# Expert products spread among the attention's small products, by a planner that counts TensorE's instructions, and a second buffer for the next pair's gram blocks

## The chip, the cores and the metric

One Trainium2 chip, one of its cores. The metric is the time of one execution on the device in microseconds; each time given for a kernel is the median of several runs.

## What is computed

Three layers follow each other on 4 x 768 = 3072 tokens. Everything is float32.

```python
def _attn_ref(q, k, v, beta):            # 4 batches, 8 heads, 768 steps, 48 wide
    k_n = k / (np.linalg.norm(k, axis=-1, keepdims=True) + 1e-06)
    for t in range(S):
        y[:, :, t] = np.einsum('bhd,bhde->bhe', q[:, :, t], state)
        v_old = np.einsum('bhde,bhd->bhe', state, kt)
        state = state + bt[:, :, :, None] * np.einsum('bhd,bhe->bhde', kt, vt - v_old)

def _moe_ref(x, w_gate, w1, w2):         # 3072 x 384, 8 experts, 1024 wide
    logits = x @ w_gate
    P = np.exp(logits - logits.max())
    for _ in range(8):
        P /= P.sum(1, keepdims=True) + 1e-09
        P /= P.sum(0, keepdims=True) + 1e-09
        P *= N / E
    for e in range(E):
        out += P[:, e:e + 1] * (np.maximum(x @ w1[e], 0.0) @ w2[e])

def _moe2_ref(x, w1, w2, w3, w_out):     # 3072 x 384, 1024 wide
    return (((x @ w1) * (x @ w2)) @ w3) @ w_out
```

## The kernel before

**Attention.** The 768 steps are cut into 12 chunks of 64, and two chunks make a pair. For a chunk, the products within it are computed at once for all 32 heads, in groups of small products that are packed four at a time into TensorE's array. `quads` (L494) issues such a group: 32 calls, which the chip executes as 64 matmuls with 64 weight loads. A chunk has seven groups:

- `gram` (L472): keys by keys, for the triangular system of the chunk. ScalarE and VectorE write its blocks into "a" (tile `a0`, L484 and the scalar_tensor_tensor after it) and "g" (tile `g12`).
- `pmm` (L648): keys by queries, masked by VectorE into "pt".
- `ks` and `qs` (L696, L705): the state by keys and by queries. `qs` starts the sum in PSUM that `pu` ends.
- `um` (L711): the inverse by the values; ScalarE writes "u". `um2` (L724): the new state; ScalarE writes "st". `pu` (L732): the output of the chunk, which goes through `xst` and DRAM (`xs_d`) and comes back token by token as `xr`.

The system of a pair is inverted by VectorE (`invert`, L507): a transposition into `asys` (L518), 14 small steps, 24 products and sums over up to 1024 columns, and a transposition of the result `t` back into `asys` (L578). Then `tt_make` (L583) forms the off-diagonal blocks: `xm` (L601) multiplies "g" with the inverse, ScalarE writes it back into the other half of "g", and `om` (L622) multiplies that once more; each is 16 calls per half chunk, executed as 32 matmuls. `gram` of the next pair writes "g" again, of which there is one buffer (`NG12 = 1`), so it comes after `om` of the pair before. The state goes from chunk to chunk through ks, um and um2.

**Expert 0.** While the attention runs, the first expert is already applied to the chunks that are finished (`e0`, L772): 24 products m1 (`xr` by the first weights) and 24 products m2 (`hA` by the second) per chunk, each of three matmuls of 128 x 128 by 256 columns. ScalarE and VectorE write `hA` (relu, split into two parts for precision), in tiles of two blocks, four buffers. The router's logits (`lg`, `lt2`) belong to each chunk as well. After the last chunk, `sinkhorn` (L901) does its eight rounds on VectorE, each with one small matmul for the sum over partitions.

**The rest.** Experts 1 to 7 follow in three passes over the tokens (`unit`, L982, with `hB` and `hA`), then the third layer (`phase_c`). Both hold TensorE with products of 512 or 384 columns.

**The order.** Nothing of this is executed in the order in which it is written. The program's operations are collected by `Plan.op` with a cost per engine, a priority and the keys that they read and write; `Plan.order` (L139) then steps through a model of the engines, takes at each moment the operation of the best priority that could start, and writes out one fixed order. `e0`'s products have priority 200 + chunk, the attention's groups -100 + chunk, the preparation of a pair (gram, inversion, xm, om, pmm) 10 times the pair and a little more. So expert products are taken where no attention operation is ready. The costs are constants of the source: `QUAD = .12` us for four calls of a group, `act` and `dve` for ScalarE and VectorE by columns. An operation marked `low` (xm, om) is put back when much of that kind ran just before.

SP's queue issues most loads and stores (L365) in the planned order: keys (`kt`), queries (`qt`, three buffers, `NQ = 3`), values, the way of the outputs through DRAM, and the stores of expert 0's results (`yr`).

Of the kernel before, what the change touches and what calls it, by code (L numbers as in the profile page):

```python
# [12 lines left out]
ALU = mybir.AluOpType  # L13
# [13 lines left out]
NKN = 2  # L27
NQ = 3
NA0 = 2
# [15 lines left out]
NC0 = 11  # L45
NG12 = 1
QUAD = .12
FLAT = "p a b c d -> p (a b c d)"
# [24 lines left out]
class Op:  # L73
    __slots__ = ("engs", "fn", "prio", "preds", "succs", "npred", "slots", "est", "rdy", "low", "start", "end", "eng", "lat", "nbytes", "hook")


class Plan:
# [14 lines left out]

    def op(self, engs, fn, r=(), w=(), prio=0.0, lat=0.0, nbytes=0, hook=None, low=False):
        o = Op()
        o.hook = hook
        o.low = low
        o.engs, o.fn, o.prio, o.lat, o.nbytes = engs, fn, (prio, len(self.ops)), lat, nbytes
# [24 lines left out]
        return o  # L122

    AHEAD = .2
    LOWMAX = 1.2
    URGENT = 2.0

    def wait_for(self, o, e, pool, now, room):
# [10 lines left out]
    def order(self):  # L139
# [11 lines left out]
        warm = {}  # L151
        lows = []

        def cost_of(o, e):
# [4 lines left out]
            if k not in warm:  # L159
# [6 lines left out]
                warm[k] = w  # L166
            return o.engs[e] * (1.0 if warm[k] else self.COLD)

        def crowded():
# [23 lines left out]
        while pool:  # L193
# [6 lines left out]
            for o in pool:  # L200
# [87 lines left out]
def act(n, psum=False):  # L288
    return (n / 1.2 + (55 if psum else 95)) / 1000

# [21 lines left out]
class Kernel:  # L312
# [123 lines left out]
    def prep_k(self, c):  # L436
# [13 lines left out]
        if st:  # L450
# [15 lines left out]
            g.op({"DVE": 1.3}, newton, r=n0 + ["bm"], w=["n1", ("bm", j), ("nv", j)], prio=pr)  # L466
        gi = j % NG12
        if st == 0:
            self.a0[j] = self.aring.new()
        sg = [self.psum.new("attn") for _ in range(2)]  # L470

        def gram(e):  # L472
            kt = lambda r, x, y, m: T["kt"][r, k.at, 8 * y + m]
            self.quads([self.ps(s, 8, 64) for s in sg], kt, kt, lambda x, y: (x, y, x), rows=D)
        g.op({"PE": 8 * QUAD}, gram, r=[k], w=sg + [(self.a0[j], "z")] + [
            (n, gi, st, hf) for n in ("g12", "xsb0", "xsb1") for hf in range(2)], prio=pr)
        for hf in range(2):
# [5 lines left out]
            g.op({"ACT": act(256, True)}, lambda e, s=s, ss=ss, a0=a0: self.copy(  # L483
                "ACT", T["a0"][:, a0.at, ss], self.ps(s, 8, 64)[:, :, 0:32], T["masks"][:, 64:65]), r=[s, "masks"], w=[ak], prio=pr)  # L484
            g.op({"ACT": act(256, True)}, lambda e, s=s, gs=gs, st=st: self.copy(
                "ACT", T["g12"][:, gi, st, gs], self.ps(s, 8, 64)[:, :, 32:64], -1.0),
                r=[s], w=[(n, gi, st, hf) for n in ("g12", "xsb0", "xsb1")], prio=pr)
            g.op({"DVE": dve(256)}, lambda e, s=s, ss=ss, a0=a0: self.stt(
                T["a0"][:, a0.at, ss], self.ps(s, 8, 64)[:, :, 32:64], T["masks"][:, 65:66], T["a0"][:, a0.at, ss], ALU.mult, ALU.add),
                r=[s, "masks", ("g12", gi, st, hf)], w=[ak], prio=pr)  # L490

# [91 lines left out]
    def tt_make(self, c):  # L583
# [8 lines left out]
        for hf in range(2):  # L592
# [15 lines left out]
            g.op({"PE": 16 * .027}, xm, r=[("g12", gi, st, hf), "asys"], w=[s], prio=pr, low=True)  # L608
            for b in range(2):
# [19 lines left out]
            g.op({"PE": 16 * .043}, om, r=[("xsb0", gi, st, hf), ("xsb1", gi, st, hf), tk(1)], w=[s2], prio=pr, low=True)  # L629
            for b in range(2):  # L630
# [5 lines left out]
    def prep_q(self, c):  # L636
# [14 lines left out]
        g.op({"PE": 8 * QUAD}, pmm, r=[q, k], w=sp + [(self.PT[c, hf], "z") for hf in range(2)], prio=pr)  # L651
        for hf in range(2):
# [15 lines left out]
    def seq(self, c):  # L668
# [24 lines left out]
        if c > 0:  # L693
            sk = two()

            def ks(e):  # L696
                self.quads([self.ps(s, 8, D) for s in sk], lambda r, x, y, m: T["kt"][r, k.at, 8 * y + m],
                           lambda r, x, y, m: T["st"][r, px.at, 8 * (x ^ y) + m], lambda x, y: (x, y, x), rows=D)
            g.op({"PE": 8 * QUAD}, ks, r=[k, (px, 0), (px, 1)], w=sk, prio=pr)
            for hf in range(2):  # L700
# [13 lines left out]
        g.op({"PE": 8 * QUAD}, um, r=vk + [(tt, hf, i) for hf in range(2) for i in range(3)] + [("qs", c)], w=su, prio=pr)  # L714
        for hf in range(2):
# [3 lines left out]
        if c < NCH - 1:  # L719
# [7 lines left out]
            g.op({"PE": 8 * QUAD * .8}, um2, r=uk + [kr], w=ss, prio=pr)  # L727
            for hf in range(2):
# [43 lines left out]
    def e0(self, c):  # L772
# [7 lines left out]
        for f0 in range(0, EB, 2):  # L780
# [4 lines left out]
            for fi in range(n):  # L785
                for kk in range(3):
                    def m1(e, kk=kk, s=s, f=f0 + fi, fi=fi):
# [113 lines left out]
    def sinkhorn(self):  # L901
# [4 lines left out]
        op("DVE", 0.0, lambda e: None, [("lgr", t) for t in range(NCH)], ["p"])  # L906
        op("DVE", .3, lambda e: nc.vector.tensor_reduce(out=cs()[:, 0:1], in_=p(), axis=AX.XY,
                                                        op=ALU.max), ["p"], ["cs"])
# [8 lines left out]
                                                        op0=ALU.mult), [s2], ["cs"])  # L917
        op("ACT", .4, lambda e: nc.scalar.activation(out=p(), in_=p(),
                                                      func=AF.Exp, bias=cs()[:, 1:2]), ["cs"], ["p"])
        for it in range(8):  # L920
            op("DVE", .3, lambda e: nc.vector.tensor_reduce(out=rs(), in_=T["p"][:, 0:NTT], axis=AX.X, op=ALU.add), ["p", "eps"], ["rs"])
            op("DVE", .1, lambda e: nc.vector.reciprocal(out=rs(), in_=rs()), [], ["rs"])
            op("DVE", .3, lambda e: self.tt("DVE", p(), p(), rs().rearrange("p (t o) -> p t o", o=1).to_broadcast([128, NTT, NE]),
                                            ALU.mult), ["rs"], ["p"])
            op("DVE", .3, lambda e: nc.vector.tensor_reduce(out=cs(), in_=T["p"][:, :, 0:NE].rearrange("p t e -> p e t"), axis=AX.X,
                                                            op=ALU.add), ["p", "eps"], ["cs"])
            s = self.psum.new("attn")
            op("PE", .2, lambda e, s=s: self.mm(self.ps(s, NE), T["ones"], cs(), start=True, stop=True), ["cs", "ones"], [s])
            op("DVE", .1, lambda e, s=s: nc.vector.reciprocal(out=cs(), in_=self.ps(s, NE)), [s], ["cs"])
            op("DVE", .3, lambda e: self.stt(p(), p(), float(NT) / NE, cs().rearrange("p (o e) -> p o e", o=1).to_broadcast(  # L930
                [128, NTT, NE]), ALU.mult, ALU.mult), ["cs"], ["p"])
# [528 lines left out]
```

## Time and profile before

| | |
|---|---|
| median of 3 runs | 2201.05 us (2196.92 to 2206.56) |
| the profiled execution, time | 2200.67 us |
| its span, first to last instruction | 2198.9 us |
| TensorE busy | 2064.0 us (94%) |
| VectorE, ScalarE, GpSimd busy | 1250.1, 716.2, 833.4 us |
| attention, expert 0 and sinkhorn, to the first product of expert 1 | 0 to 490.3 us |
| experts 1 to 7 | 490.3 to 1917 us |
| third layer | 1917 to 2198.9 us |

In rows of the profile PE is TensorE's matmuls, PEld its weight loads, DVE VectorE, ACT ScalarE, POOL GpSimd, SP the queue of SyncE. Times are microseconds from the start of the span. "PEclk" is the granted clock of TensorE as a share of 2.4 GHz; at 0.5 it runs at 1.2 GHz. Nearly all matmuls have the line L334, that of a helper, so they are told apart by what they read: `kt` alone is gram, `qt,kt` pmm, `st,kt` ks, `qt,st` qs, `vs,tt` um, `u,kraw` um2, `pt,u` pu, `asys,g` xm, `tt,g` om, `xr,wA` m1, `hA,wA` m2, `xr,wg` and `masks,yr` the logits, `cs,ones` the sinkhorn's sums, `xT,...` expert 1 and later.

### The profile page before, as it was taken

How to read it: one execution, taken by the hardware profiler on the slowest of the kernel's cores; microseconds unless marked ns; L12 is line 12 of the kernel's file. 1: busy time of each engine (PE TensorE's matmuls, PEld its weight loads, DVE VectorE, ACT ScalarE, POOL GpSimd, SP SyncE). 2: the span in 40 equal slices, each digit the busy share in tenths (PEclk: the TensorE clock that was granted, in tenths of full speed). 3: DMA queues.
4: the chain of work that ended last, by engine and by line, in shares of the span. 5: the costliest groups of instructions: out<-in, count | busy, mean ns of one | idle time of the engine just before them, and what ended most of it. 6: DMA issues, size and time to landing. Idle time of an engine off the chain costs nothing.

```text
span 2198.9 us, 39139 instructions
## 1 busy us (share of the span) xinstructions
PE 2064.0 (94%) x16017; PEld 1761.6 (80%) x16017; DVE 1250.1 (57%) x1957; ACT 716.2 (33%) x1387; POOL 833.4 (38%) x893
## 2 busy tenths in 40 slices
PE   2889998888999899989999999999999999999999
PEld 1878887876888787778887788788887888988888
DVE  7867765553545555576666766767667644222222
ACT  3433333333344334333233233323322322222222
POOL 3200000034766856754546544634466434300000
PEclk9899978899999999999999999999999999999999
DMA  6432131135555555684556445555655545700000
GB/s 218 156 106 72 64 96 53 41 104 199 204 195 191 182 178 201 210 286 164 206 201 232 163 176 199 199 179 196 211 206 172 206 142 164 139 29 30 15 15 30
DMA packets 165461, 331.61 MB, mean 151 GB/s; under 512 B 13280, under 2 KB 117664, under 8 KB 153760
## 3 DMA queue, kind: packets, MB, share of 16 engines
q1 hardware_dynamic: 131392, 193.82, 26.8%
q0 software_dynamic: 33888, 135.28, 17.9%
q8 instruction: 126, 2.06, 0.4%
q14 instruction: 55, 0.45, 0.1%
HBM read 235.10 MB, written 93.95 MB: 150 GB/s over the span
## 4 chain that ended last, share of the span: by engine, by line
PE 78%; DVE 6%; issue 5%; POOL 4%; DMA 4%; ACT 2%; SPq 1%; POOLq 0%; DVEq 0%; ACTq 0%
PE b L334 78%; DMA rawB<-in_moe_w 2%; DVE prod L345 1%; POOL acc L345 1%; POOL wA L345 1%; SPq L365 1%; POOL wS L345 1%; POOL rawB L345 1%; DVE cv L348 1%; DVE t L544 0%; DVE xs L544 0%; DMA xst<-xs_d 0%; DMA wA<-wq_d 0%; ACT rt L338 0%; DVE hA L348 0%
## 5 line engine op out<-in xcount | busy, mean ns | idle before, releaser
L334 PE MATMUL b<-hA,wA 128*128 128x512 f32 (+1 forms) x2367 | 502.9, 354 | 5.9 <-DVE hA L348 3.5
L334 PEld LDWEIGHTS b<-hA,wA 128*128 128x128 f32 x2367 | 392.9, 191 | 67.1 <-DVE hA L348 4.7
L334 PE MATMUL b<-hB,wA 128*128 128x512 f32 x1521 | 391.5, 393 | 2.3 <-DVE hB L348 2.3
L345 POOL TENSOR_TENSOR acc<-acc,tmp 128x512 f32<-128x512 f32 x252 | 331.2, 1316 | 160.4 <-DVE tmp L345 157.6
L334 PEld LDWEIGHTS b<-hB,wA 128*128 128x128 f32 x1521 | 288.1, 189 | 63.6 <-DVE hB L348 3.5
L334 PE MATMUL b<-xr,wA 128*128 128x256 f32 (+1 forms) x1620 | 326.9, 340 | 0.0
L334 PEld LDWEIGHTS b<-xr,wA 128*128 128x128 f32 x1620 | 255.1, 195 | 31.6 <-DVE b L345 0.4
L345 DVE TENSOR_TENSOR tmp<-b,pb 128x512 f32<-128x512 f32 x234 | 161.0, 689 | 200.1 <-PE b L334 192.4
L338 ACT ACTIVATE rt<-b 128x512 f32<-128x512 f32 x300 | 178.0, 597 | 256.6 <-PE b L334 250.9
L334 PE MATMUL b<-xT,wA 128*128 128x512 f32 x1008 | 253.7, 393 | 6.8 <-ACT wA L338 5.6
L345 DVE TENSOR_TENSOR b<-b,rt 128x512 f32<-128x512 f32 x252 | 173.8, 696 | 125.1 <-ACT rt L338 62.2
L334 PEld LDWEIGHTS b<-xT,wA 128*128 128x128 f32 x1008 | 190.4, 189 | 49.0 <-ACT wA L338 6.4
L334 PE MATMUL b<-xT,wS 128*128 128x512 f32 x756 | 205.0, 396 | 16.7 <-ACT wS L338 9.2
L345 POOL TENSOR_TENSOR cv<-cv 128x256 f32<-128x256 f32 (+3 forms) x175 | 127.7, 730 | 198.9 <-DVE cv L1222 109.6
L334 PEld LDWEIGHTS b<-xT,wS 128*128 128x128 f32 x756 | 141.1, 189 | 55.2 <-ACT wS L338 12.5
L348 DVE SCALAR_TENSOR_TENSOR hA<-b,hA 128x512 fp32r<-128x512 f32 x215 | 144.7, 689 | 58.5 <-ACT hA L1032 41.5
L345 DVE TENSOR_TENSOR rt<-b,rt 128x512 f32<-128x512 f32 x48 | 33.2, 692 | 186.0 <-PE b L334 186.0
L1032 ACT ACTIVATE hB<-b 128x512 fp32r<-128x512 f32 x169 | 100.5, 597 | 108.6 <-DVE b L345 106.0
L348 DVE SCALAR_TENSOR_TENSOR hB<-b,hB 128x512 fp32r<-128x512 f32 x169 | 115.3, 686 | 34.7 <-ACT hB L1032 34.4
L345 POOL TENSOR_TENSOR wA<-rawB,wA 128x768 fp32r<-128x768 f32 (+2 forms) x64 | 95.9, 1507 | 102.4 <-ACT wA L338 76.3
L338 ACT ACTIVATE cv<-cv 128x256 fp32r<-128x256 f32 x72 | 29.2, 405 | 281.8 <-DVE cv L348 281.8
L1032 ACT ACTIVATE hA<-b 128x512 fp32r<-128x512 f32 x167 | 97.6, 597 | 57.9 <-DVE b L345 32.9
(164 smaller groups left out, 2425.3 us busy)
## 6 DMA issues: line engine op xcount, KB each, us to landing
wA<-wq_d POOLq DMA_DIRECT2D x56, 1536.0 KB, 9.2
wq_d<-wA SPq DMA_DIRECT2D x28, 1536.0 KB, 7.0
wS<-ws_d POOLq DMA_DIRECT2D x56, 512.0 KB, 5.7
rawB<-in_moe_w SPq DMA_DIRECT2D x112, 192.0 KB, 4.3
ws_d<-wS SPq DMA_DIRECT2D x28, 512.0 KB, 4.3
w_d<-cv SPq DMA_DIRECT2D x112, 128.0 KB, 2.1
pb<-p_d SPq DMA_DIRECT2D x42, 256.0 KB, 4.2
cvr<-in_w3T SPq DMA_DIRECT2D x32, 256.0 KB, 2.7
```

The source lines that it names most:

```text
L334: self.nc.tensor.matmul(*args, skip_group_check=True, **kw)
L338: self.nc.scalar.activation(out=out, in_=in_, func=AF.Copy, **({} if scale is None else {"scale": scale}))
L345: self.E[eng].tensor_tensor(out=out, in0=in0, in1=in1, op=op)
L348: self.nc.vector.scalar_tensor_tensor(out=out, in0=in0, scalar=scalar, in1=in1, op0=op0, op1=op1)
L365: return self.g.op({eng: cost}, lambda _: e.dma_start(out=out(), in_=in_()), r=r, w=w, prio=prio, nbytes=nbytes, lat=lat)
L1032: g.op({"ACT": actb(512)}, lambda e: nc.scalar.activation(out=hv(0), in_=self.ps(s, 512), func=AF.Relu), r=[s], w=[(out, 0, 0)], prio=pe)
```

## The change

Four things change, all of them ahead of the code that runs on the chip, except two buffers.

1. The planner counts TensorE's instructions. Each operation has a number `ins` (6 unless given: three matmuls and three weight loads; 128 for a group, 32 for xm and om). `fetch` says by how much the instruction that stands 256 further along would come too early, 3.9 us after the one 256 before it. A group (16 instructions or more) that would wait by more than 0.1 us is put back, and the next best operation that can start, in most cases an expert product, is taken. What is late all the same is added to the group's time.
2. `NG12` is 2, and `gram` with the four operations behind it has priority -120 + pair from the second pair on, ahead of the attention. Its place is paid for by the third query buffer (`NQ` 3 to 2).
3. `qs` of a chunk reads a key that `pu` of the chunk before writes, so it stands behind it.
4. Costs are set anew: `QUAD` .12 to .14, 55 ns more for each operation of ScalarE, m1 .33 to .36, the sinkhorn's steps each for itself.

```diff
-NQ = 3
+NQ = 2
...
-NG12 = 1
-QUAD = .12
+NG12 = 2
+QUAD = .14
...
+    BLOCK = 256
+    FETCH = 3.9
...
+        def fetch(o, now):
+
+            if o.ins < 16:
+                return 0.0
+            d = 0.0
+            for x in (0.0, .5, 1.0):
+                i = issued[0] + x * o.ins - self.BLOCK
+                for i0, n, a, b in reversed(stream[-300:]):
+                    if i0 <= i < i0 + n:
+                        d = max(d, a + (b - a) * (i - i0) / n + self.FETCH - now - x * o.engs["PE"])
+                        break
+            return d
...
-                if o.low and full:
+                if o.low and full or e == "PE" and fetch(o, now) > .1:
                     spare = spare or (o, e)
                     continue
...
+            if e == "PE":
+                late = fetch(o, now)
+                end += late
+                stream.append((issued[0], o.ins, now + late, end))
+                issued[0] += o.ins
...
-    return (n / 1.2 + (55 if psum else 95)) / 1000
+    return (n / 1.2 + (110 if psum else 150)) / 1000
...
+        pg = pr if j == 0 else -120.0 + j
...
-        g.op({"PE": 8 * QUAD}, gram, r=[k], w=sg + [(self.a0[j], "z")] + [
-            (n, gi, st, hf) for n in ("g12", "xsb0", "xsb1") for hf in range(2)], prio=pr)
+        g.op({"PE": 8 * QUAD}, gram, ins=128, r=[k], w=sg + [(self.a0[j], "z")] + [
+            (n, gi, st, hf) for n in ("g12", "xsb0", "xsb1") for hf in range(2)], prio=pg)
...
-            g.op({"PE": 8 * QUAD}, qs, r=[q, (px, 0), (px, 1)], w=sy + [("qs", c)], prio=pr)
+            g.op({"PE": 8 * QUAD}, qs, ins=128, r=[q, (px, 0), (px, 1), ("pu", c - 1)], w=sy + [("qs", c)], prio=pr)
...
-        g.op({"PE": 8 * QUAD}, pu, r=uk + pts, w=sy + [(xb, "z")], prio=pr + .2)
+        g.op({"PE": 8 * QUAD}, pu, ins=128, r=uk + pts, w=sy + [(xb, "z"), ("pu", c)], prio=pr + .2)
...
-                    g.op({"PE": .33}, m1, r=xk + [("w", f0 + fi, i) for i in range(2)], w=[s, (h, "z")], prio=pr)
+                    g.op({"PE": .36}, m1, r=xk + [("w", f0 + fi, i) for i in range(2)], w=[s, (h, "z")], prio=pr)
...
-        op("ACT", .4, lambda e: nc.scalar.activation(out=p(), in_=p(),
+        op("ACT", 1.75, lambda e: nc.scalar.activation(out=p(), in_=p(),
```

What this does to the order is seen at two places. On TensorE, in the middle of the attention, the end of um2 and what follows it. Before, it is the next group:

```order
L334 MATMUL b_141<-u,kraw 48x48 x2
L334 MATMUL b_137<-u,kraw 48x48 x2
L334 MATMUL b_141<-u,kraw 48x48
L334 MATMUL b_135<-pt,u 48x64 x2
L334 MATMUL b_134<-pt,u 48x64 x2
```

And with the change, at such a place:

```order
L357 MATMUL b_137<-u,kraw 48x48 x2
L357 MATMUL b_136<-u,kraw 48x48
L357 MATMUL b_134<-xr,wA 128x256 x12
L357 MATMUL b_140<-hA,wA 128x256 x6
L357 MATMUL b_138<-st,kt 64x48 x2
```

Four products m1 and two m2 stand between um2 and ks, where before one group followed the other.

The second place is VectorE's, between the end of one pair's inversion (the transposition of t into asys) and the start of the next (that of a into asys). Before, for the third and the fourth pair ("a<-b" writes the next pair's gram blocks, "vs<-b" follows ks, "tt" are the off-diagonal blocks):

```order
L578 STREAM_TRANSPOSE asys<-t 128x32x32
L580 STREAM_TRANSPOSE a_113<-t 128x32x32
...
L345 TENSOR_TENSOR vs<-vs,nv 128x768
L348 SCALAR_TENSOR_TENSOR vs<-b_138,vs 128x384
L348 SCALAR_TENSOR_TENSOR vs<-b_140,vs 128x384
L348 SCALAR_TENSOR_TENSOR a_113<-b_135,masks,a_113 128x256
L348 SCALAR_TENSOR_TENSOR a_113<-b_136,masks,a_113 128x256
L348 SCALAR_TENSOR_TENSOR a_113<-b_135,masks,a_113 128x256
...
L345 TENSOR_TENSOR xr<-xst,xr 128x768
L348 SCALAR_TENSOR_TENSOR a_113<-b_136,masks,a_113 128x256
L518 STREAM_TRANSPOSE asys<-a_113 128x1024
```

With the change, for the fourth and the fifth pair:

```order
L602 STREAM_TRANSPOSE asys<-t 128x32x32
L604 STREAM_TRANSPOSE a_113<-t 128x32x32
L371 SCALAR_TENSOR_TENSOR hA<-b_139,hA 128x512
L368 TENSOR_TENSOR tt<-a_113,bm 128x8x32 x2
L368 TENSOR_TENSOR tt<-b_139,bm 32x8x32 x2
L368 TENSOR_TENSOR tt<-b_140,bm 32x8x32 x2
L371 SCALAR_TENSOR_TENSOR hA<-b_134,hA 128x512
L368 TENSOR_TENSOR tt<-b_139,bm 32x8x32 x2
L542 STREAM_TRANSPOSE asys<-a_113 128x1024
```

The gram blocks were written during the inversion before; the operations on the state (vs) come after the start of the next one.

## Rows read from the trace of the kernel before

**Rows 1.** Busy time by stretch: from:to, length; each engine (instructions); PEclk, DMA share, GB/s

```profile
50.80:126.10 75.30, 67.14 (x1436) 62.87 (x1436) 65.02 (x118) 30.89 (x68) 12.38 (x7) 0.89 0.39 121
126.10:197.00 70.90, 61.59 (x1460) 58.41 (x1460) 49.31 (x79) 23.84 (x55) 3.58 (x4) 0.93 0.30 88
197.00:269.00 72.00, 65.53 (x1484) 62.31 (x1483) 47.99 (x74) 24.35 (x57) 2.24 (x2) 0.91 0.29 90
269.00:338.00 69.00, 62.75 (x1489) 59.71 (x1488) 49.91 (x75) 24.27 (x57) 3.59 (x3) 0.83 0.26 79
338.00:410.00 72.00, 64.43 (x1474) 60.70 (x1474) 48.03 (x74) 23.85 (x55) 1.65 (x4) 0.91 0.15 46
410.00:490.30 80.30, 67.23 (x1009) 62.16 (x1003) 37.01 (x82) 25.35 (x51) 13.85 (x11) 0.85 0.30 86
...
520.30:1917.00 1396.70, 1368.09 (x5999) 1126.68 (x6000) 837.00 (x1303) 464.87 (x883) 754.74 (x823) 0.99 0.57 193
```

**Rows 2.** Timeline of TensorE, 208 to 229 us: first and last of six stops

```profile
208.15 0.51 PE L334 MATMUL b<-u,kraw 64*48 64x48 f32 x26 [1.02 <-issue]
...
228.72 0.66 PE L334 MATMUL b<-qt,st 48*48 48x64 f32 x29 [0.95 <-issue]
```

**Rows 3.** The page: TensorE's instructions, the instruction queue, loads of qt

```profile
PE 2064.0 (94%) x16017; PEld 1761.6 (80%) x16017; DVE 1250.1 (57%) x1957; ACT 716.2 (33%) x1387; POOL 833.4 (38%) x893
...
q8 instruction: 126, 2.06, 0.4%
...
qt<-in_qT SPq DMA_DIRECT2D x12, 512.0 KB, 5.0
```

**Rows 4.** Timeline of TensorE: operations at full clock, the last at a lower one

```profile
197.01 1.20 PE L334 MATMUL b<-asys,g 32*32 32x32 f32 x64
...
204.36 1.15 PE L334 MATMUL b<-vs,tt 64*64 64x48 f32 x64
205.44 0.69 PE L334 MATMUL b<-tt,g 32*32 32x32 f32 x32
...
229.31 0.87 PE L334 MATMUL b<-xr,wg 128*16 128x256 f32 x6
...
296.88 1.91 PE L334 MATMUL b<-st,kt 48*64 48x48 f32 x64
```

**Rows 5.** Busy time in slices of 10 us, columns as in rows 1

```profile
180.00:190.00 10.00, 10.00 (x86) 10.00 (x85) 9.79 (x10) 2.08 (x5) 0.00 (x0) 1.00 0.12 39
...
290.00:300.00 10.00, 7.86 (x290) 7.23 (x284) 6.20 (x10) 2.69 (x5) 2.40 (x1) 0.50 0.46 140
```

**Rows 6.** Waits of TensorE, 50.5 to 490 us: us in total, times, longest

```profile
PE b L334 <- issue: 36.4, 28, 2.8
...
PE b L334 <- DVE cs L925: 6.7, 5, 2.2
...
PE b L334 <- DMA qt<-in_qT: 0.3, 1, 0.3
```

**Rows 7.** VectorE from one inversion's end to the next start; last, two groups' means

```profile
194.76 2.06 DVE L578 STREAM_TRANSPOSE asys<-t 128x1024 f32<-128x1024 f32 x1
...
217.51 0.48 DVE L348 SCALAR_TENSOR_TENSOR a<-b,masks,a 128x256 f32<-128x256 f32 x1 [3.92 <-ACT g L338]
...
229.62 2.00 DVE L518 STREAM_TRANSPOSE asys<-a 128x1024 f32<-128x1024 f32 x1
...
L348 DVE SCALAR_TENSOR_TENSOR hA<-b,hA 128x512 fp32r<-128x512 f32 x42 | 28.8, 686 | 10.7 <-ACT hA L796 10.5
...
L345 DVE TENSOR_TENSOR prod<-a,xs 128x1024 f32<-128x1024 f32 x18 | 23.5, 1322 | 0.0
```

**Rows 8.** Timeline of TensorE: the last pu, and the sinkhorn's result transposed

```profile
431.28 2.33 PE L334 MATMUL b<-pt,u 64*48 64x64 f32 x64 [0.59 <-ACT u L338]
...
479.98 0.38 PE L1174 MATMUL b<-ident,tmp 128*96 128x128 f32 x2
```

**Rows 9.** Waits of SP's queue, 0 to 450 us: us in total, times, longest

```profile
SPq L365 <- ACT yr L338: 207.0, 21, 22.0
```

More of the change, by code (lines that the diff above doesn't have):

```diff
@@ L73 @@
 class Op:
-    __slots__ = ("engs", "fn", "prio", "preds", "succs", "npred", "slots", "est", "rdy", "low", "start", "end", "eng", "lat", "nbytes", "hook")
+    __slots__ = ("engs", "fn", "prio", "preds", "succs", "npred", "slots", "est", "rdy", "low", "start", "end", "eng", "lat", "nbytes", "hook", "ins")
 class Plan:
@@ L91, in __init__, with op @@
         self.rd = {}
-    def op(self, engs, fn, r=(), w=(), prio=0.0, lat=0.0, nbytes=0, hook=None, low=False):
+    def op(self, engs, fn, r=(), w=(), prio=0.0, lat=0.0, nbytes=0, hook=None, low=False, ins=6):
         o = Op()
@@ L96, in op @@
         o.low = low
+        o.ins = ins
         o.engs, o.fn, o.prio, o.lat, o.nbytes = engs, fn, (prio, len(self.ops)), lat, nbytes
@@ L152, in order @@
         lows = []
+        stream = []
+        issued = [0]
         def cost_of(o, e):
@@ L483, in prep_k @@
             g.op({"ACT": act(256, True)}, lambda e, s=s, ss=ss, a0=a0: self.copy(
-                "ACT", T["a0"][:, a0.at, ss], self.ps(s, 8, 64)[:, :, 0:32], T["masks"][:, 64:65]), r=[s, "masks"], w=[ak], prio=pr)
+                "ACT", T["a0"][:, a0.at, ss], self.ps(s, 8, 64)[:, :, 0:32], T["masks"][:, 64:65]), r=[s, "masks"], w=[ak], prio=pg)
             g.op({"ACT": act(256, True)}, lambda e, s=s, gs=gs, st=st: self.copy(
                 "ACT", T["g12"][:, gi, st, gs], self.ps(s, 8, 64)[:, :, 32:64], -1.0),
-                r=[s], w=[(n, gi, st, hf) for n in ("g12", "xsb0", "xsb1")], prio=pr)
+                r=[s], w=[(n, gi, st, hf) for n in ("g12", "xsb0", "xsb1")], prio=pg)
             g.op({"DVE": dve(256)}, lambda e, s=s, ss=ss, a0=a0: self.stt(
                 T["a0"][:, a0.at, ss], self.ps(s, 8, 64)[:, :, 32:64], T["masks"][:, 65:66], T["a0"][:, a0.at, ss], ALU.mult, ALU.add),
-                r=[s, "masks", ("g12", gi, st, hf)], w=[ak], prio=pr)
+                r=[s, "masks", ("g12", gi, st, hf)], w=[ak], prio=pg)
     TDONE = [("t16", 1, 0), ("t16", 1, 8), ("t16", 0)]
@@ L607, in xm @@
                                 start=True, stop=True, tile_position=(64 * b, 64 * b + 32))
-            g.op({"PE": 16 * .027}, xm, r=[("g12", gi, st, hf), "asys"], w=[s], prio=pr, low=True)
+            g.op({"PE": 16 * .027}, xm, r=[("g12", gi, st, hf), "asys"], w=[s], prio=pr, low=True, ins=32)
             for b in range(2):
@@ L628, in om @@
                                 start=True, stop=True, tile_position=(64 * b + 32, 64 * b))
-            g.op({"PE": 16 * .043}, om, r=[("xsb0", gi, st, hf), ("xsb1", gi, st, hf), tk(1)], w=[s2], prio=pr, low=True)
+            g.op({"PE": 16 * .043}, om, r=[("xsb0", gi, st, hf), ("xsb1", gi, st, hf), tk(1)], w=[s2], prio=pr, low=True, ins=32)
             for b in range(2):
@@ L650, in pmm @@
                        lambda r, x, y, m: T["qt"][r, q.at, 8 * y + m], lambda x, y: (x, x ^ y, x), rows=D)
-        g.op({"PE": 8 * QUAD}, pmm, r=[q, k], w=sp + [(self.PT[c, hf], "z") for hf in range(2)], prio=pr)
+        g.op({"PE": 8 * QUAD}, pmm, ins=128, r=[q, k], w=sp + [(self.PT[c, hf], "z") for hf in range(2)], prio=pr)
         for hf in range(2):
@@ L698, in ks @@
                            lambda r, x, y, m: T["st"][r, px.at, 8 * (x ^ y) + m], lambda x, y: (x, y, x), rows=D)
-            g.op({"PE": 8 * QUAD}, ks, r=[k, (px, 0), (px, 1)], w=sk, prio=pr)
+            g.op({"PE": 8 * QUAD}, ks, ins=128, r=[k, (px, 0), (px, 1)], w=sk, prio=pr)
             for hf in range(2):
@@ L713, in um @@
                        lambda r, x, y, m: T["vs"][r, v.at, 8 * x + m], lambda x, y: (y, x ^ y, y))
-        g.op({"PE": 8 * QUAD}, um, r=vk + [(tt, hf, i) for hf in range(2) for i in range(3)] + [("qs", c)], w=su, prio=pr)
+        g.op({"PE": 8 * QUAD}, um, ins=128, r=vk + [(tt, hf, i) for hf in range(2) for i in range(3)] + [("qs", c)], w=su, prio=pr)
         for hf in range(2):
@@ L726, in um2 @@
                            lambda r, x, y, m: T["u"][r, u.at, 8 * y + m], lambda x, y: (x ^ y, x, x ^ y), cols=D, first=c == 0)
-            g.op({"PE": 8 * QUAD * .8}, um2, r=uk + [kr], w=ss, prio=pr)
+            g.op({"PE": 8 * QUAD * .8}, um2, ins=128, r=uk + [kr], w=ss, prio=pr)
             for hf in range(2):
@@ L906, in sinkhorn @@
         op("DVE", 0.0, lambda e: None, [("lgr", t) for t in range(NCH)], ["p"])
-        op("DVE", .3, lambda e: nc.vector.tensor_reduce(out=cs()[:, 0:1], in_=p(), axis=AX.XY,
+        op("DVE", .37, lambda e: nc.vector.tensor_reduce(out=cs()[:, 0:1], in_=p(), axis=AX.XY,
                                                         op=ALU.max), ["p"], ["cs"])
@@ L917, in sinkhorn @@
                                                         op0=ALU.mult), [s2], ["cs"])
-        op("ACT", .4, lambda e: nc.scalar.activation(out=p(), in_=p(),
+        op("ACT", 1.75, lambda e: nc.scalar.activation(out=p(), in_=p(),
                                                       func=AF.Exp, bias=cs()[:, 1:2]), ["cs"], ["p"])
         for it in range(8):
-            op("DVE", .3, lambda e: nc.vector.tensor_reduce(out=rs(), in_=T["p"][:, 0:NTT], axis=AX.X, op=ALU.add), ["p", "eps"], ["rs"])
-            op("DVE", .1, lambda e: nc.vector.reciprocal(out=rs(), in_=rs()), [], ["rs"])
-            op("DVE", .3, lambda e: self.tt("DVE", p(), p(), rs().rearrange("p (t o) -> p t o", o=1).to_broadcast([128, NTT, NE]),
+            op("DVE", .4, lambda e: nc.vector.tensor_reduce(out=rs(), in_=T["p"][:, 0:NTT], axis=AX.X, op=ALU.add), ["p", "eps"], ["rs"])
+            op("DVE", .32, lambda e: nc.vector.reciprocal(out=rs(), in_=rs()), [], ["rs"])
+            op("DVE", .5, lambda e: self.tt("DVE", p(), p(), rs().rearrange("p (t o) -> p t o", o=1).to_broadcast([128, NTT, NE]),
                                             ALU.mult), ["rs"], ["p"])
-            op("DVE", .3, lambda e: nc.vector.tensor_reduce(out=cs(), in_=T["p"][:, :, 0:NE].rearrange("p t e -> p e t"), axis=AX.X,
+            op("DVE", .54, lambda e: nc.vector.tensor_reduce(out=cs(), in_=T["p"][:, :, 0:NE].rearrange("p t e -> p e t"), axis=AX.X,
                                                             op=ALU.add), ["p", "eps"], ["cs"])
@@ L928, in sinkhorn @@
             op("PE", .2, lambda e, s=s: self.mm(self.ps(s, NE), T["ones"], cs(), start=True, stop=True), ["cs", "ones"], [s])
-            op("DVE", .1, lambda e, s=s: nc.vector.reciprocal(out=cs(), in_=self.ps(s, NE)), [s], ["cs"])
-            op("DVE", .3, lambda e: self.stt(p(), p(), float(NT) / NE, cs().rearrange("p (o e) -> p o e", o=1).to_broadcast(
+            op("DVE", .22, lambda e, s=s: nc.vector.reciprocal(out=cs(), in_=self.ps(s, NE)), [s], ["cs"])
+            op("DVE", .42, lambda e: self.stt(p(), p(), float(NT) / NE, cs().rearrange("p (o e) -> p o e", o=1).to_broadcast(
                 [128, NTT, NE]), ALU.mult, ALU.mult), ["cs"], ["p"])
```

## Prediction

> **What bounds the kernel.** I began with the busy time by stretch [rows 1]. From 520.3 us on, TensorE works 1368.1 of 1396.7 us, and the third layer behind it looks no different: the end of the program is set by TensorE, and there the change reorders little. The room lies ahead of 490.3 us. The stretches are cut where the four "xm" of a pair start (50.8, 126.1, 197, 269, 338, 410 us) and where expert 1 starts (490.3). In the five pair stages TensorE is idle for 6 to 9 us of some 70, and VectorE for 10 to 24.
>
> Next, TensorE's instructions in time [rows 2]. Where only small products follow each other, TensorE stops in the middle of an operation, and the stop is put down to "issue": nothing that the trace shows released it. Counted out between the two rows, 126 to 128 matmuls lie from one stop to the next, with as many weight loads 256 instructions. The page's DMA section has 126 packets on the instruction queue, and TensorE alone has 16017 matmuls and 16017 weight loads [rows 3]: 32034 by 126 is 254, so one packet feeds 256 TensorE instructions. From the stop that ends at 208.15 to the one that ends at 228.72 are five blocks in 20.57 us; I take 4.1 us as the least time of a block. 64 small matmuls run in 1.08 us (204.36 to 205.44 [rows 4]), 128 instructions; two such operations use up a block in 2.2 us and then wait. A product of expert 0, three matmuls, takes 0.36 us (86 matmuls in 10 us, 0.35 a product, at best [rows 5]) and only six instructions.
>
> Third, what else holds TensorE. Of its waits from 50.5 to 490 us [rows 6], "issue" has 36.4 us and the sinkhorn's sums 6.7. Where small products stand alone the granted clock falls too, to 0.50, 1.2 GHz, in the slice from 290 us [rows 5]; 64 small matmuls then take 1.91 us (296.88 [rows 4]).
>
> Last, VectorE [rows 7]. The inversion of a pair ends with the transposition at 194.76. The next begins only at 229.62, since the four "a" operations ahead of it (from 217.51 on) wait for the next pair's gram. Until then VectorE is mostly idle.
>
> **The sum.** I counted TensorE's operations in both orders between the same marks and priced them by rows at full clock [rows 4, 5]: 1.08 us an operation of 64 matmuls, 0.60 an xm or om half (two in 1.20 us, 197.01), 0.36 an expert product, 0.87 each of the two steps of the logits (229.31). Then I cut the sequence into blocks of 256 instructions and added what each lacks of 4.1 us.
>
> Before: 340.2 us of work; 41 of 65 blocks are too short and lack 72.4 us. By stage that makes 71.0, 70.4, 72.5, 68.1, 69.8 and 60.9, where the stretches took 75.3, 70.9, 72.0, 69.0, 72.0 and 80.3 [rows 1]. So the count gives the middle stages to within 2.2 us (mean 0.8) and the first to 4.3; the last has 19.4 us more, from waits for the last chunk's way through DRAM, the sinkhorn and a clock of 0.85.
>
> After: the same work; 22 of 65 blocks are too short and lack 20.8 us (13.2 in the first pair's stage, where at first no expert product is ready). By stage: 56.0, 49.7, 49.0, 48.4, 52.0 and 105.8, together 360.9. Stages 1 to 5 shrink for two reasons: the blocks are fed, and 124 expert products leave them (341 of 465 stay, and the last stage's 111 become 235), since the next inversion no longer waits and the pairs come sooner.
>
> VectorE must keep up with that. Its instructions between two inversion ends, each at the mean duration of its kind up to 450 us, come to 72.4, 53.1, 51.9, 51.2 and 51.8 us before, where it was busy 65.0, 49.3, 48.0, 49.9 and 48.0 [rows 1]: a factor of 0.93, for records that overlap. After they come to 68.4, 52.3, 48.2, 46.8 and 48.7, by that factor 64, 49, 45, 44 and 45. The inversion, 31.6 us of each, is unchanged; but in the last three stages no "a" operation stands any longer between the end of one and the start of the next, 7 to 11 rows of the order in all.
>
> The larger of the two engines by stage is 64.0, 49.7, 49.0, 48.4, 52.0 and 105.8: 368.9 us. Two engines that are both nearly full take turns in waiting. To the 0.8 us that the count missed I add 2, some 3 us for each of five stages and 3 for the last: 386.9. With the first 50.8 us, unchanged, expert 1 starts at 437.7 us instead of 490.3: **53 us less**. The profiled execution took 2200.67 us, 0.4 below the median of 2201.05; from the median I predict **2148 us**.
>
> **The other parts.** The last stage: 188 expert products stand behind the last pu, 67.7 us, where the chain from pu's end (433.6) to the sinkhorn's transposed result (480.4) took 47 us [rows 8]; it is covered, and the 6.7 us of sinkhorn waits go. Without that cover they stay, which the upper end holds. The third query buffer given up: no load of qt held TensorE above 0.3 us [rows 6], a load lands in 5.0 us [rows 3], and two buffers still leave it a chunk's time, half a stage of 50 us; nothing at best, ten loads by 5.0 us if each came late. I take nothing, the lead being five loads long. The grams that move ahead need their keys a pair's attention earlier; there are four key buffers, and the next pair's two were read last in the pair before. The bounds are the same 0 to 5.0 us a pair, and I take nothing for the same reason. What these loads pass on SP's queue is a rival below; POOL's queue keeps its work. That qs now follows pu of the chunk before adds no wait: both stand on TensorE's queue, which runs in order, and um behind qs is later than that pu anyhow. The new prices of ScalarE, sinkhorn and products change no instruction, only the order. Experts 1 to 7 and the third layer: the first units stand in the same order as before, later ones are turned by a step here and there; 28.6 us are idle there [rows 1], of which a third either way, 10 us, is my bound; I take nothing, since the amount of work is the same.
>
> **A rule against it.** The stops come once per 256 TensorE instructions [rows 2, 3], and by them 52 of 72 us of lacking block time can be won. The Trainium skill, page "Runtime: NRT & Kernel Launch", section "Instruction fetch mechanics", says that the queue is refilled in blocks of 256 instructions, and that the fetch is hidden because the sequencer issues more slowly than blocks arrive. By that rule none of the 52 us is there to win. The trace agrees on the blocks and not on the hiding.
>
> **Rivals.**
> *The stops belong to the small products, not to their supply.* They would then come along wherever those stand: 360.9 - 20.8 + 72.4 = 412.5, with the same 18 us of waits 430.5, and expert 1 starts at 481 us: 9 less, 2192. For it: "issue" names no releaser. Against: the even count of 256. The skill's page just named would have it so. Chance 0.06.
>
> *The engines take turns far worse.* SP's queue waited 207 us for the expert's results "yr", once 22.0 us [rows 9], and in the new order loads of keys and values stand behind such stores; or VectorE is left as idle as in the first stage before, 10 us of each [rows 1]. With 10 us instead of 3 for each of five stages, 35 more: 2183. Chance 0.20.
>
> *Slower.* Second products need hA, which ScalarE and VectorE write, and VectorE now has the inversion's operations, 1.3 us the longest [rows 7], nearly all the time. A product stuck in TensorE's queue holds up the attention behind it. Stages 1 to 5 hold 173 first products, 29 hA tiles; one takes 0.69 us on VectorE, I suppose as much on ScalarE ahead of it, and 1.3 to get past an operation, 2.7 us, and 78 us if TensorE sits through all of it: 2226. It decides from 53/29 = 1.8 us a tile on. Against: of TensorE's waits none above 0.3 us names hA [rows 6], though second products ran beside the inversion before too. Chance 0.05.
>
> *Forecast*: 0.69. At its lower end the engines take no turns (18 us) and the later phases give 10: 2120.
>
> **Numbers.** A measurement of this kernel can tell about 0.5%, 11 us, from no change. Below 2190 lie the forecast and 0.18 of the turns: 0.87 faster. From 2190 to 2212 the first rival and the rest of the turns: 0.08. Above: 0.05. The range, 2118 to 2184, leaves out the first rival, the slower one and the worse part of the turns.
>
> **What would show it.** Right: the first product of expert 1 near 438 us; pair stages of 50 to 55 us after a first one near 67; "issue" waits of TensorE under 15 us; a granted clock near 1.0 from 126 us on; inversions that start within 12 us of the end of the one before; no idle TensorE in the sinkhorn. Wrong: stages near 70 us with "issue" unchanged (first rival), waits for hA (slower), SP waits ahead of kt or kraw (turns), or later phases that are longer by over 10 us.

## The result, and the profile after

| | before | with the change |
|---|---|---|
| median | 2198.99 us (4 runs, 2192.07 to 2206.56) | 2137.4 us (4 runs, 2133.49 to 2142.45) |
| ratio, 95% interval | | 0.9721 [0.9681, 0.976] |
| the profiled execution: time, span, mean granted clock | 2200.67 us, 2198.9 us, 0.971 | 2133.49 us, 2131.3 us, 0.991 |
| first product of expert 1 | 490.3 us | 433.9 us |

The change makes the kernel faster by 61.6 us by the medians; 53 were forecast. Between the two profiled executions it is 67.2 us, of which 56.4 lie ahead of expert 1.

Busy time by stretch of the kernel after, columns as in [rows 1], cut at the same marks: the first "xm" of each pair, then the first product of expert 1.

```profile
50.10:115.60 65.50, 54.53 (x1444) 50.58 (x1444) 62.54 (x109) 30.48 (x69) 7.92 (x6) 0.90 0.45 138
115.60:166.90 51.30, 51.13 (x1283) 47.50 (x1282) 48.76 (x82) 22.34 (x52) 5.55 (x6) 1.00 0.33 95
166.90:218.20 51.30, 50.01 (x1374) 45.55 (x1373) 44.68 (x70) 19.72 (x49) 5.75 (x5) 1.00 0.42 121
218.20:270.50 52.30, 50.38 (x1269) 45.98 (x1269) 46.95 (x67) 20.28 (x47) 9.38 (x6) 1.00 0.31 96
270.50:322.30 51.80, 50.89 (x1382) 46.19 (x1381) 44.94 (x69) 20.09 (x48) 1.37 (x2) 1.00 0.31 91
322.30:433.90 111.60, 109.18 (x1589) 104.67 (x1589) 49.04 (x100) 36.65 (x74) 16.20 (x13) 1.00 0.22 64
```

Read the length first, then TensorE's busy time against it, then the granted clock (third from the end). The middle stages last 51.3 to 52.3 us instead of 69 to 72, and TensorE is idle in them for 0.2 to 1.9 us. The six stages together last 383.8 us, where those of [rows 1] last 439.5. TensorE's busy time in them falls from 388.7 to 366.1 us and its idle time from 50.8 to 17.7: of the 55.7 us, 33.1 are idle time and 22.6 are the same work done in less time, at a clock of 1.00 instead of 0.83 to 0.93 (1.00 is 2.4 GHz).

Waits of TensorE after, 50 to 440 us (us in total, times, longest), beside [rows 6]:

```profile
PE b L357 <- DVE asys L602: 34.8, 2, 34.4
PE b L357 <- DVE vs L371: 5.3, 1, 5.3
PE b L357 <- issue: 3.7, 7, 1.1
...
PE b L357 <- DVE cs L949: 1.6, 3, 0.7
```

The first row is the wait for the first inversion, whose end falls at the window's start; it belongs to the first 50 us of both kernels. "issue" falls from 36.4 to 3.7 us, and that difference, 32.7, is nearly the whole loss of idle time. The timeline of TensorE after shows why, 150.79 to 161.16 us:

```profile
150.79 1.15 PE L357 MATMUL b<-vs,tt 64*64 64x48 f32 x64
151.87 2.05 PE L357 MATMUL b<-xr,wA 128*128 128x256 f32 x15
153.85 0.94 PE L357 MATMUL b<-u,kraw 64*48 64x48 f32 x64
154.72 0.62 PE L357 MATMUL b<-xr,wA 128*128 128x256 f32 x3
155.18 1.60 PE L357 MATMUL b<-hA,wA 128*128 128x256 f32 x12
156.70 1.11 PE L357 MATMUL b<-pt,u 64*48 64x64 f32 x64
157.75 2.41 PE L357 MATMUL b<-xr,wA 128*128 128x256 f32 x18
160.08 1.15 PE L357 MATMUL b<-st,kt 48*64 48x48 f32 x64
```

Every group of 64 small matmuls has products of expert 0 on both sides, and no row has an idle time ahead of it.

Last, VectorE after, from an inversion's end to the next start, twice (beside [rows 7]):

```profile
164.05 2.08 DVE L602 STREAM_TRANSPOSE asys<-t 128x1024 f32<-128x1024 f32 x1
179.25 1.94 DVE L542 STREAM_TRANSPOSE asys<-a 128x1024 f32<-128x1024 f32 x1
...
216.23 1.95 DVE L602 STREAM_TRANSPOSE asys<-t 128x1024 f32<-128x1024 f32 x1
228.37 1.99 DVE L542 STREAM_TRANSPOSE asys<-a 128x1024 f32<-128x1024 f32 x1
```

Between them lie 13.1 and 10.2 us, where [rows 7] show 32.8. Over all five the gaps are 16.9, 12.8, 13.1, 10.2 and 13.0 us instead of 30.4, 32.0, 32.8, 20.9 and 23.7.

### The profile page after: what moved, and what is told of

The parts are those of the page before. It is cut to its first block, busy times and chain, and to the rows that moved or that the text cites. A ratio compares the mean times of both kernels' runs of the same rounds, so it can differ in the third digit from the quotient of the medians.

```text
span 2131.3 us, 39119 instructions
## 1 busy us (share of the span) xinstructions
PE 2034.6 (95%) x16017; PEld 1734.2 (81%) x16017; DVE 1245.0 (58%) x1950; ACT 712.8 (33%) x1384; POOL 843.3 (40%) x903
## 3 DMA queue, kind: packets, MB, share of 16 engines
q1 hardware_dynamic: 131392, 193.82, 27.6%
## 4 chain that ended last, share of the span: by engine, by line
PE 79%; DVE 7%; DMA 5%; POOL 4%; issue 3%; ACT 1%; SPq 1%; DVEq 0%; POOLq 0%; ACTq 0%
PE b L357 79%; DMA rawB<-in_moe_w 2%; DVE prod L368 1%; SPq L388 1%; POOL wA L368 1%; DMA kt<-in_kT 1%; POOL acc L368 1%; DVE cv L371 1%; POOL rawB L368 1%; POOL wS L368 1%; DVE b L368 1%; DVE hA L371 0%; DMA w_d<-cv 0%; DVE t L568 0%; DMA wA<-wq_d 0%
## 5 line engine op out<-in xcount | busy, mean ns | idle before, releaser
L368 POOL TENSOR_TENSOR cv<-cv 128x256 f32<-128x256 f32 (+2 forms) x177 | 129.1, 729 | 190.6 <-DVE cv L1246 111.4
L368 DVE TENSOR_TENSOR rt<-b,rt 128x512 f32<-128x512 f32 x48 | 33.2, 692 | 186.0 <-PE b L357 186.0
L1056 ACT ACTIVATE hA<-b 128x512 fp32r<-128x512 f32 x167 | 97.0, 597 | 50.8 <-DVE b L368 28.8
```

Source lines behind the costliest of these rows:

```text
L368: self.E[eng].tensor_tensor(out=out, in0=in0, in1=in1, op=op)
L1056: g.op({"ACT": actb(512)}, lambda e: nc.scalar.activation(out=hv(0), in_=self.ps(s, 512), func=AF.Relu), r=[s], w=[(out, 0, 0)], prio=pe)
```

## The experiments

My theory was the prediction's: TensorE is supplied with 256 instructions at a time, at least some 4.1 us apart; spreading the small groups among products feeds the blocks; the early inversion brings the pairs sooner. The rivals: the stops belong to the small products themselves; the early inversion alone is the whole gain; counting alone is.

### The stops by themselves

A kernel that holds nothing but series of matmuls:

In outline:

```python
group(b, n)    # 64 matmuls with 64x64 weights, n columns, packed four at a time
product(n, b)  # n times three matmuls of 128x128 by 256 columns
# A: 12 x group(48)                     B: 12 x group(256)
# C: 12 x (group(48), product(6))       D: 24 x group(48), 16 loads of 1.5 MB on SP's queue
```

> This kernel computes nothing of the layers and writes zeros; it issues four series on TensorE, with long products of 512 columns between them: A, 12 groups of 64 small matmuls (48 columns) one behind the other; B, the same 12 groups with 256 columns; C, 12 times one group of 48 columns and behind it six products of three 256-column matmuls (164 instructions); D, 24 groups of 48 columns while SP's queue loads 16 times 1.5 MB. Theory (TensorE's instructions are supplied 256 at a time, at least 4.1 us apart): A, 6 blocks of 256, about 25 us instead of the 13 us that 12 times 1.08 us make, with a stop after every 126 to 128 matmuls; B, where a group takes some 5.8 us (1.08 times 256/48), no stops; C, no stops, 12 times 3.24 us, 39 us, since 256 instructions take 5.1 us; D, 12 blocks, 49 us or, if transfers slow the supply, more. Rival (the stops belong to the small products): stops in A and C alike, C some 12 us above 39, and their distance in C not near 256 instructions. Without the transfers of data that run in the layers the time of a block may be under 4.1 us in A and B; D against A tells that.

Its timeline of TensorE: series A from 19.02 us, B at 48.45, the first pieces of C from 99.38, and a part of D.

```profile
19.02 2.64 PE L34 MATMUL b<-f 64*64 64x48 f32 x163
22.43 2.08 PE L34 MATMUL b<-f 64*64 64x48 f32 x128 [0.76 <-issue]
26.15 2.08 PE L34 MATMUL b<-f 64*64 64x48 f32 x128 [1.65 <-issue]
30.16 2.62 PE L34 MATMUL b<-f 64*64 64x48 f32 x128 [1.92 <-issue]
33.61 5.59 PE L34 MATMUL b<-f 64*64 64x48 f32 x221 [0.83 <-issue]
...
48.45 41.67 PE L34 MATMUL b<-f 64*64 64x256 f32 x768
...
99.38 1.15 PE L34 MATMUL b<-f 64*64 64x48 f32 x64
100.46 2.40 PE L34 MATMUL b<-r 128*128 128x256 f32 x18
102.79 1.15 PE L34 MATMUL b<-f 64*64 64x48 f32 x64
...
156.53 2.70 PE L34 MATMUL b<-f 64*64 64x48 f32 x128 [3.61 <-issue]
...
179.12 2.08 PE L34 MATMUL b<-f 64*64 64x48 f32 x128 [0.89 <-issue]
185.59 3.66 PE L34 MATMUL b<-f 64*64 64x48 f32 x128 [4.39 <-issue]
...
205.99 3.66 PE L34 MATMUL b<-f 64*64 64x48 f32 x128 [1.42 <-issue]
```

In A the first stop comes behind 163 matmuls, and from then on one after exactly 128, 256 instructions with their weight loads. Only the last 221 show none: they take 5.59 us, longer than at full clock (128 in 2.08 us), and I read this as giving the next block time to come. B and C have no stop at all: the 768 matmuls of B run as one row, and in C the same 48-column groups as in A alternate with products, 12 pieces of 3.43 us in a row (39 us were expected, 41.2 came). The rival, stops that go with the small products, falls.

The windows of the same kernel, one row for each of A, B, C and D:

```profile
19.02:39.13 20.11, 14.94 (x769) 14.38 (x768) 0.00 (x0) 0.00 (x0) 0.00 (x0) 0.83 0.02 5
48.45:90.05 41.60, 41.60 (x770) 29.28 (x769) 0.00 (x0) 0.00 (x0) 0.00 (x0) 1.00 0.01 2
99.38:138.13 38.75, 38.75 (x967) 36.64 (x966) 0.00 (x0) 0.00 (x0) 0.00 (x0) 1.00 0.01 3
149.58:211.44 61.86, 37.84 (x1537) 36.29 (x1536) 0.00 (x0) 0.00 (x0) 0.00 (x0) 0.65 0.94 349
```

Series A took 20.1 us, not the 25 expected, since its blocks are 3.7 us apart ((33.61 - 22.43)/3). In D, with DMA at 0.94 of its time, nine blocks lie between 156.53 and 205.99: 5.5 us each on average. The lower clock of D does not explain it: the block at 179.12 ran at full clock, in 2.08 us, and the next came 6.47 us behind its start. So the supply slows while data is being moved; the 4.1 us of the attention lie between, at a DMA share of 0.54 in the stretch where they were read (208.15 to 228.72 us in the kernel before). And the granted clock falls with the stops: 0.83 in A and 0.65 in D, 1.00 in C, with the same groups.

### Counting and buffer, each alone

Three kernels with the new constants of cost and with `qs` behind `pu` in all of them. Without counting (second buffer and early grams kept):

```diff
-            if o.ins < 16:
-                return 0.0
+            return 0.0
```

> The changed kernel without the counting of instructions (fetch gives 0 always); second gram buffer, early grams and new costs stay. Theory (the stops are the supply of 256-instruction blocks, and both halves of the change earn): by the count of blocks in its order, priced as in the prediction, TensorE lacks 50.0 us of block time instead of 20.8, and the larger of TensorE and VectorE by stage sums to 393 us instead of 369: 24 us more, expert 1 at about 458 us instead of 433.9, about 2161 us in all; TensorE's issue waits 15 to 25 us instead of 3.7. Rival B (the stops belong to the small products themselves, all gain is the early inversion): as fast as the changed kernel, 2137. Rival C (all gain is the counting, the buffer does nothing): back near 2190.

Without the buffer (counting kept):

```diff
-NQ = 2
-NG12 = 2
+NQ = 3
+NG12 = 1
-        pg = pr if j == 0 else -120.0 + j
+        pg = pr
```

> The changed kernel with one gram buffer, three query buffers and grams at their old priority; counting and new costs stay. Theory: its order lacks 47.8 us of block time; the larger of the two engines by stage sums to 394 us, 25 more than the changed kernel, and VectorE again waits for the grams before an inversion, so 2162 to 2175 us, with VectorE's idle time ahead of the a operations back above 15 us. Rival B (only the early inversion earns): 2199, as before. Rival C (only the counting earns): 2137.

And with both of these edits:

> Neither counting nor the second buffer (one buffer, three query buffers, grams at the old priority): what is left of the change is the new constants of cost and qs behind pu. Theory as the earlier runs left it (without early grams the way from one inversion's end through xm, om and gram to the next inversion sets a stage, whatever the supply): 2190 to 2203, no change, although the block count lacks 55.5 us instead of 72.4. Rival (the lacking block time sets the stages by itself): 17 us less than before, 2185 or under.

| | median, us | ratio to before, interval | expert 1 at, us | "issue", 50 us to expert 1 | five gaps, us | five inversions, us |
|---|---|---|---|---|---|---|
| neither | 2181.98 | 0.9942 [0.992, 0.9964] | 474.4 | 33.2 | 153.1 | 198.2 |
| counting alone | 2197.43 | 0.9979 [0.9961, 0.9997] | 487.5 | 30.8 | 180.3 | 183.2 |
| buffer and early grams alone | 2166.86 | 0.984 [0.98, 0.9879] | 470.2 | 22.6 | 67.5 | 233.7 |
| both (the change) | 2137.4 | 0.9721 [0.9681, 0.976] | 433.9 | 3.7 | 66.1 | 205.6 |

A gap is the time on VectorE from the end of one inversion to the start of the next; "five inversions" are the stretches between the gaps, second to sixth pair, each from the start of an inversion to its end. Each ratio is to the kernel before, timed beside that kernel.

(The profiled run of "neither" took 2173.21, 8.8 us under its median, so its 474.4 is early.) Three things follow. The two parts don't add: counting gains some 1.2% where the early grams are there (0.984 to 0.9721) and nothing where they aren't (0.9942 to 0.9979, with intervals that just meet). My expectation for counting alone missed by over 20 us, and by the mechanism too: I had put VectorE's idle time ahead of the "a" operations above 15 us, and it is 4.8. And what is left with both out, the constants of cost and the place of `qs`, gains 0.6% (15.5 us by the medians), where I had expected nothing and the rival, by the block count, 17. The number is the rival's, but "issue" is only 3.2 us under [rows 6], so that the gain lies in the supply is not shown. In the profiled execution it lies in the clock: up to expert 1 TensorE is busy for 381.6 us instead of 396.6, at a granted clock of 0.95 instead of 0.90, 15.0 of the 15.9 us by which expert 1 starts earlier. Which of the two edits carries it was not tried.

Without counting, the early inversions work as expected (gaps of 10.6 to 19.4 us) and the stops come back: "issue" has 22.6 us, inside the 15 to 25 expected, expert 1 starts 12 us later than the 458 expected, and the time lies between the rivals' values, 6 us above the theory's.

Why does counting not pay alone? One gap of "counting alone", between the fifth pair's inversion and the sixth's, as a window, and with it the ends on VectorE and the grams on TensorE:

```profile
325.83:379.68 53.85, 52.45 (x1322) 47.85 (x1313) 19.55 (x33) 21.07 (x49) 1.37 (x2) 1.00 0.21 62
```

```profile
323.85 1.98 DVE L602 STREAM_TRANSPOSE asys<-t 128x1024 f32<-128x1024 f32 x1
379.68 1.99 DVE L542 STREAM_TRANSPOSE asys<-a 128x1024 f32<-128x1024 f32 x1
```

```profile
371.98 1.16 PE L357 MATMUL b<-kt 48*64 48x64 f32 x64
...
375.46 1.16 PE L357 MATMUL b<-kt 48*64 48x64 f32 x64
```

TensorE is busy for 52.45 of 53.85 us at full clock, so no block is short there; but VectorE has 19.55 us of work in that time, since the next pair's two grams come at 371.98 and 375.46, behind all groups of two chunks and the products that counting put between them. The gaps of that kernel are 32.8, 44.4, 27.0, 22.3 and 53.8 us, 27 us more in all than with neither part. That is one half of the answer: spreading puts products ahead of the grams, for which VectorE waits.

The other half is that the stops stay. The gap shown is the only one nearly without them; the four before it have 7.4, 8.4, 5.4 and 2.4 us of "issue", and only 8, 88, 11 and 74 matmuls of expert products to mix in. I read this as products used up beside the inversions: 261, 222, 207 and 105 of their matmuls run beside the four that follow these gaps, with 128 to 583 other matmuls beside any of the five. With late grams the groups stand in the gaps, and an inversion leaves TensorE little but products. In the change 746 to 814 other matmuls run beside each inversion, with 136 to 194 of the products', and there counting earns: it shortens the five inversions from 233.7 to 205.6 us and leaves the gaps as they are. The early grams bring groups and products together in time, and spreading then delays nothing that VectorE waits for.

### The priority of the grams

Second buffer and counting kept, the early place given up:

```diff
-        pg = pr if j == 0 else -120.0 + j
+        pg = pr
```

> The changed kernel with the second gram buffer but with the grams at the old priority, behind the attention. Theory: the buffer lets the grams go before the off-diagonal blocks are through, the priority makes them go a whole pair earlier; by the count the order lacks 30.1 us, the larger engine by stage sums to 377 us (8 more), and the last stage has only 98 expert products more than it needs none to cover the sinkhorn, so 10 us more of waits there: 2150 to 2160. If the priority is idle and the buffer alone matters: 2137. If the buffer is idle without the priority: as e2_one_buffer.

2172.2 us, 0.9866 [0.9826, 0.9907]; expert 1 at 466.16, gaps 20.1, 27.3, 26.5, 27.6 and 26.5 us, "issue" 11.9. I missed by at least 12 us again, on the same side. Beside counting, the free buffer is worth 1.1% without the early place (0.9979 to 0.9866; gaps of 20 to 28 us where counting alone has 22 to 54), so neither the case where it is idle nor the one where it does everything came. The step from 2172 to 2137 is the priority's.

### Three small terms

The count of xm and om as executed, 64 instructions instead of the 32 that the change states:

```diff
-..., prio=pr, low=True, ins=32)
+..., prio=pr, low=True, ins=64)
```

> The changed kernel with 64 instead of 32 instructions counted for an xm or om half (the chip executes 32 matmuls and 32 weight loads for one). Theory: the order lacks 18.5 us of block time instead of 20.8, the larger engine by stage sums to 370.4 instead of 368.9: no difference, 2137 within 5 us. If the wrong count costs: 3 to 5 us less.

2146.41 us, 0.975 [0.9716, 0.9783], expert 1 at 445.8 us: no gain from the truer number. By the medians it is 9 us above the changed kernel, outside of my 5; by the ratios the two are not told apart, since the intervals overlap.

The old constants of cost (`QUAD`, `act`, m1 and the sinkhorn's steps as before), the rest as changed:

> The new constants of cost go back to those of before, while counting, buffer and early grams stay. Theory: the constants only turn the order; block count 367.9 us instead of 360.9 for the six stages, VectorE's chain the same, so expert 1 near 441 us and 2144 us, bounds 2137 to 2156 (the later phase may turn by 12 us either way). Rival: the constants carry the gain of the later phase and some of the stages: 2160 or more.

2149.04 us, 0.9779 [0.9753, 0.9806], expert 1 at 449.5 us: within the bounds, 5 us above the value (expert 1 8.5 us later than forecast). Against the change it is 0.6% by the middles, about what the constants and `qs` gave above, with intervals that just meet, so the gain is not clear of noise; the rival's 2160 is out.

The third query buffer kept beside the second gram buffer:

```diff
-NQ = 2
+NQ = 3
```

> The third query buffer is kept beside the second buffer of the gram blocks; all else as changed. Theory (two query buffers are enough, priced at nothing): block count 360.1 instead of 360.9, so 2137, bounds 2131 to 2145. Rival (loads of queries come late with two): up to ten loads by 5.0 us, 2090 to 2125, and waits for qt that vanish.

2142.77 us, 0.9761 [0.9734, 0.9787], expert 1 at 439.7. That is 6 us above the value and within the bounds: two buffers cost nothing that shows, as priced; the rival falls. The words on the change have its place "paid for" by the third buffer: this kernel has room for both, so the payment was not needed.

## Why the prediction was right

**The bound.** The stops were read rightly: 256 instructions a block, and the block time as the scarce thing. The 4.1 us are not the least time of a block, though, but a mean at the DMA share of one stretch (0.54); series A has 3.7. "Issue" went below the 15 us that I named. Of the clock I had only said that it would be near 1.0 from 126 us on, and had priced the work at full clock on both sides; it came so, and 22.6 of the 55.7 us of the six stages show up there, as the same work in less time. Series A and C show the link: with the stops the clock falls, without them it stays. In my count both lay in one sum, since a block that is short by the count can as well be filled by matmuls at the lower level (1.91 us instead of 1.08 for 64, [rows 4]).

**The stages.** Forecast, with the turns, 67.0, 52.7, 52.0, 51.4, 55.0 and 108.8 us; they took 65.5, 51.3, 51.3, 52.3, 51.8 and 111.6. VectorE's share came as counted: 64, 49, 45, 44 and 45 us forecast, 62.5, 48.8, 44.7, 47.0 and 44.9 measured. Two sizes inside the sum were off and cancelled. The work on TensorE, 340.2 us by my prices, took 366.1. The price of a product held: after the change, too, it is 0.36 us in a long run (54 matmuls, 18 products, in 6.48 us):

```profile
427.42 6.64 PE L357 MATMUL b<-hA,wA 128*128 128x256 f32 x54
433.90 2.41 PE L357 MATMUL b<-xT,wA 128*128 128x512 f32 x9
```

What I had put at nothing is the change from small groups to products. A run of products between two groups takes some 0.18 us more than 0.36 a product, whether it holds five (1.98 us, 151.87 to 153.85 above) or six (2.33, 157.75 to 160.08; likewise 2.33 in series C). The change makes many such runs: in the four stages from 115.6 to 322.3 us I count some 80, with 15 us in all. The other large part lies in the first pair's stage, where the granted clock was 0.90: its small groups took about 10 us more than at full clock. Against these 26 us stand waits of 17.7 us in place of 46.7 (386.9 - 340.2): TensorE's longer time feeds the blocks too, which I read as the reason that little of the 20.8 us of lacking block time shows, and the turns cost 0.2 to 3.0 us a stage (length less the busier engine's time) instead of 3. That the two cancel to 3 us is in part luck.

**The start of expert 1**: 437.7 forecast, 433.9 came.

**Later phases.** Taken as 0 with 10 either way. In the profiled executions they are 11 us shorter: from expert 1's start to the end 1708.6 us before and 1697.4 after. By the medians only about 5 us are left for them (61.6 - 56.4), since the profiled execution after is the fastest of its four. One place carries most of the 11, 400 to 500 us behind expert 1's start; the windows of before and of after:

```profile
890.27:990.27 100.00, 90.89 (x370) 71.80 (x369) 65.42 (x92) 39.86 (x78) 65.44 (x73) 0.95 0.75 260
```

```profile
833.90:933.90 100.00, 94.95 (x410) 77.48 (x409) 68.61 (x103) 37.52 (x73) 59.33 (x64) 0.98 0.71 242
```

40 more matmuls run there after the change, with 4 us less idle time and a granted clock of 0.98 instead of 0.95. Before, TensorE waited at three points in that window for over 2 us, each time for a tile that another engine writes; after, at one, 4.0 us for hA. The first and the last of the three:

```profile
911.66 1.23 PE L334 MATMUL b<-hA,wA 128*128 128x512 f32 x3 [2.46 <-ACT hA L1032]
...
954.06 0.80 PE L334 MATMUL b<-hB,wA 128*128 128x512 f32 x1 [2.28 <-DVE hB L348]
```

The length of this phase is 1697 us with both parts out and 1709 with counting alone, so neither part sets it; I read it as a turn of the planned order, and no run tested that.

**The rivals.** *Stops of the small products*: refuted by series C. The Trainium skill, page "Runtime: NRT & Kernel Launch", section "Instruction fetch mechanics", has the fetch hidden behind a slower sequencer. The blocks of 256 that it states agree with series A, the hiding does not: 0.8 to 1.9 us of stop a block there, and up to 4.4 in D. *Far worse turns*: SP's queue waits 117.9 us for "yr" (22 times, the longest 16.6) instead of 207.0 [rows 9], and no turn is over 3.0 us. *Slower through hA*: the delay exists, but in VectorE. Its waits after, 50 to 440 us:

```profile
DVE hA L371 <- ACT hA L820: 23.0, 18, 4.8
```

TensorE has no wait for hA over 0.2 us in the same window; that enough other products stood ahead of the late ones is my reading.

**What fell short.** Of the marks set, two were missed by a little: the inversions start 10.2 to 16.9 us behind the end of the one before, not within 12, and TensorE still waits 1.6 us for the sinkhorn's sums, where no wait was forecast. And the step that would have failed had it been asked is the one on the parts: the prediction gives two reasons why "stages 1 to 5 shrink", and my expectations for the parts alone took them as two that add. The runs show that the early grams are the condition for the other.

## What to carry to other kernels

When an engine stops where nothing releases it, count its instructions from stop to stop: a number that stays the same points at the supply, and then mixing operations that last long for few instructions among those that last short is worth the stops and the clock that falls with them. Before spreading, look at two things: whether filler and small operations are ready at the same time, and what the operations that are put back lead to. Filler on the way to a step that another engine waits for moves the loss there, so first give that step a buffer and an early place. Test such parts alone and together, since here one of them was worth nothing without the other.

## What the runs showed of the hardware

The time of a block of 256 TensorE instructions is no constant: 3.7 us with the DMA engines nearly idle (share 0.02), 4.1 in the attention at a share of 0.54, 5.5 at 0.94. A planner's single number of 3.9 fits a moderate load only. The reserve ahead of the stops is small as well: behind 60 matmuls of 512 columns the first stop of series A came after 163 small matmuls; that of D, behind 18 of 256 columns and 40 of 512, after 211. And a change from small groups to products costs TensorE 0.18 us each time, however long the run of products is: spreading has a price, some 15 us in the four middle stages here.
